# Softcap attention followed by a gated MLP on one core: two small loads change queue, two weight loads move behind accumulating transfers, and the hand-written order of the attention passes is written anew

## The chip, the core and the metric

One Trainium2 chip, one core. The metric is the device time of one execution in microseconds (us); lower is better. Times are those of the profiler or of the timed runs of this kernel.

## What is computed

```python
# q, k, v: (4, 12, 448, 64) float32; cap: one number; w_in: (768, 2048); w_out: (2048, 768)
scores = (q @ k^T) / sqrt(64)
scores = cap * tanh(scores / cap)
attn = exp(scores - max); attn = attn / (sum(attn) + 1e-9)
x = (attn @ v) as (1792, 768)          # tokens by heads x head_dim
h = x @ w_in
out = (h * sigmoid(h)) @ w_out         # (1792, 768)
```

## The kernel before

Everything is scheduled by hand: each engine executes its own list of instructions in the order in which the code issues them, and waits only where data, a buffer or a PSUM bank is not ready. A step that is issued earlier or later in the code stands earlier or later in the list of its engine.

**Attention** runs in 12 passes (numbered `s`, 0 to 11). A pass handles two pairs of heads: `QK` tiles hold queries and keys of a pair (four buffers, two per pass), `VT` and `VB` the values. The keys of a pass are cut into seven units `u` (0 to 6). The steps are written as short names, `name.pass` in the tables `START` and `END`, and `name+lag` or `name-lag` in `SLOT`, which is repeated for each pass in `MIDDLE`:

- `Qu`: the four TensorE products of unit `u` (line 327) into a tile `s` of two PSUM banks. There are three such tiles, used in turn.
- `Tu`: ScalarE reads the tile and writes tanh into `P` (line 336), which frees the tile.
- `E0`, `E1`, `E2`: ScalarE's exp over units 0 to 2, 3 to 5, and 6 (line 340); `eu` is the exp of one unit, used in the first and the last pass.
- `Vu`: TensorE multiplies values with `P` into the tile `o` (line 387). There is only one such tile (two banks), so that the first `V` of a pass waits until `N0` of the pass before has read it.
- `S0` to `S4` and `A0`: the row sums. `S0` adds units 0 and 1, `S1` units 3 and 4, `S4` adds unit 5, `S2` unit 6, `S3` adds both halves, all on VectorE (lines 356 to 365). `A0` adds unit 2 to the first half: in passes 1 to 10 by an accumulating transfer on GpSimd's queue (line 370, `T<-P` in the rows), in passes 0 and 11 by VectorE. `S3` therefore waits for that transfer.
- `SUM`: TensorE sums over the partitions with a matrix of ones, into a tile `s` (line 397). It waits for `S3`.
- `UT0`, `UT1`, `UT2`: VectorE transposes, takes the reciprocal, transposes back (lines 408, 411, 414). `UT0` frees the tile of `SUM`.
- `N0`, `N1`, `N2`: VectorE divides and splits the result into a high and a low part, `XH` and `XL` (lines 425 to 429).
- `D1`, `D2`: VectorE decodes pieces of the MLP's first weights, which come as 64-bit words in `RAW` (lines 167 to 180, 615, 640).
- `LQ`, `LV`: loads of queries and keys two passes ahead, and of values one pass ahead, on SyncE's queue. A `QK` buffer is free when the last `Q` of the pass that used it is done.
- `H0` to `H5`: six parts of the first MLP product, placed into the last pass.

The loads of the first two pieces of `w_out` (768 KB as seen in the profile) go into the `RAW` buffers of the first two pieces of `w_in` as soon as these are decoded: the decode puts them on a list `WANTED`, and `LQ` issues what stands there behind its own loads, on SyncE's queue.

Ahead of `START` stand the first loads: queries and keys of pairs 0 and 1 in two pieces each, `cap` into `cap0` and, for partition 64, into `cap64`, values, pairs 2 and 3, two pieces of `w_in`. `setup3`, issued behind the first `T`, makes the small constant `epst` from `cap0` and `cap64` with two exps on ScalarE (lines 274 and 275), the second of which needs `cap64`; ScalarE's first exp of the pass, line 340, stands behind them.

**The MLP** follows, ordered by a planner in the code (`plan`), line 760 and line 870 in the profile. Its products use PSUM tiles `A` to `D` (one bank each) and `q` (two of two banks), which take over the banks of `s` and `o`.

Of the kernel before, what the change touches and what calls it, by code (L numbers as in the profile page):

```python
# [185 lines left out]
def tile_softcap_attention_swish_moe(  # L186
# [12 lines left out]
    nc = tc.nc  # L199
# [5 lines left out]
    S = NT // B  # L205
# [3 lines left out]
    KW = KF + 128  # L209
# [22 lines left out]
    psm = ExitStack()  # L232
    pool = lambda st, name, bufs, **kw: st.enter_context(tc.tile_pool(name=name, bufs=bufs, reuse_waits="tile", **kw))
# [18 lines left out]
    cap64 = a1.tile([128, 1], F32, name="cap64")  # L252
# [54 lines left out]
    def load_qk(i, c0=0, c1=S + KW, eng=nc.sync):  # L307
        eng.dma_start(out=QK[i % 4][:, c0:c1], in_=qkv[i, :, c0:c1])
# [108 lines left out]
    def norm(s, parts=(0, 1, 2)):  # L417
# [37 lines left out]
    }  # L455

    START = """
        Q0.0 Q1.0 Q6.0 T0.0 Q3.0 e0.0 T1.0 T6.0 e1.0 Q4.0 T3.0 Q5.0 T5.0 D1.1 Q2.1 T4.0 Q2.0 Q0.1 T2.1 D2.1 e3.0
        e5.0 e4.0 Q1.1 V3.0 V1.0 LV.0 T2.0 T0.1 S0.0 V5.0 e6.0 V4.0 T1.1 LQ.0 e2.0 D1.2 S1.0 Q4.1 Q3.1 T3.1 S4.0
        Q5.1 A0.0 T4.1 V0.0 T5.1 S3.0 V2.0 V6.0 D2.2 SUM.0 E0.1 D1.3 UT0.0 Q1.2 E1.1 T1.2 Q4.2 T4.2 Q6.1 T6.1  # L460
        LQ.1 Q2.2 T2.2 Q0.2 UT1.0 S0.1 Q5.2 E2.1 T0.2 UT2.0 S1.1 T5.2 N0.0 V0.1 V3.1 D2.3 V1.1 S2.0 E0.2 D1.4
        Q3.2 LV.1 S2.1 V2.1 S4.1 Q2.3 A0.1 V6.1 S3.1 SUM.1 T3.2 S0.2 Q6.2 T2.3 LQ.2 V4.1 N1.0 V5.1 Q1.3 E1.2
        UT0.1 UT1.1 Q0.3 UT2.1 T6.2 A0.2 T1.3 Q4.3 T0.3 E2.2 S1.2 Q3.3 E0.3 T4.3 N0.1 S4.2 S2.2 Q5.3 V1.2 N2.0
        V6.2 T5.3 S3.2 S0.3 V5.2 T3.3 LV.2 V2.2 V0.2 SUM.2 V3.2 UT0.2 Q2.4 Q6.3 E1.3 T2.4 N1.1 Q1.4 V4.2 T6.3
        T1.4 UT1.2 UT2.2 E2.3 Q0.4 T0.4 Q4.4 LQ.3 Q3.4 LV.3 S1.3 N0.2 V3.3 Q5.4 V5.3 T4.4 S4.3 A0.3 V6.3 D2.4
        E0.4 S2.3 N1.2 S3.3 N2.1 V0.3 V1.3 T3.4 SUM.3 V2.3 S0.4 Q6.4 T5.4 Q2.5 E1.4 UT0.3 V4.3 LQ.4 T6.4 UT1.3
        Q0.5 Q1.5 T2.5 T0.5 D1.5
    """.split()
# [8 lines left out]
    END = """
        T1.9 UT2.7 E2.8 Q4.9 Q3.9 LV.8 S1.8 N0.7 V3.8 T4.9 V2.8 V4.8 S4.8 Q5.9 N2.6 S2.8 V0.8 T3.9 A0.8 E0.9
        T5.9 D2.9 Q6.9 S3.8 V6.8 SUM.8 T6.9 E1.9 LQ.9 Q2.10 V1.8 S0.9 V5.8 N1.7 UT0.8 Q1.10 Q4.10 T2.10 T1.10
        T4.10 E2.9 Q5.10 Q0.10 Q6.10 T5.10 UT1.8 UT2.8 N2.7 N0.8 V0.9 LV.9 S1.9 T0.10 E0.10 Q3.10 V6.9 V2.9 S2.9  # L480
        T6.10 V1.9 A0.9 D1.10 S4.9 V5.9 S3.9 T3.10 E1.10 S0.10 SUM.9 Q2.11 A0.10 V3.9 UT0.9 UT1.9 T2.11 V4.9
        LQ.10 UT2.9 N0.9 S1.10 Q4.11 Q1.11 T4.11 Q3.11 S4.10 Q0.11 T1.11 E2.10 V2.10 e1.11 D2.10 V0.10 S2.10
        V6.10 S3.10 S2.11 V4.10 N1.8 V1.10 T3.11 Q6.11 LV.10 T0.11 e2.11 N2.8 SUM.10 V3.10 e3.11 UT0.10 Q5.11
        V5.10 e0.11 UT1.10 S0.11 UT2.10 H0 e4.11 H1 LQ.11 T5.11 e5.11 H2 N1.9 T6.11 N0.10 S1.11 H3 H4 H5 A0.11
        V5.11 V3.11 S4.11 LV.11 V2.11 V1.11 S3.11 N1.10 N2.9 V4.11 N2.10 e6.11 SUM.11 UT0.11 UT1.11 V0.11 V6.11
        UT2.11 N0.11
    """.split()

    def step(op, s):
        if not 0 <= s < NS:  # L490
            return
        j = int(op[-1]) if op[-1].isdigit() else None
        if op == "SUM":
            pv_sum(s)
        elif op[:2] == "UT":
            u_sums(s, j)
        elif op[0] == "N":
            if s + 1 < NS or j == 0:
                norm(s, (j,))
        elif op[0] == "D":  # L500
            if (s, op) in FIRST:
                decode(*FIRST[s, op])
        elif op[0] == "A":
            fold(s)
        elif op == "LQ":
            if s + 2 < NS:
                load_qk(2 * s + 4)
                load_qk(2 * s + 5)
            for m in WANTED:
                load_w(m)  # L510
            WANTED.clear()
        elif op == "LV":
            if s + 1 < NS:
                load_v(s + 1)
                if (s + 1) % NU == 0:
                    load_rem((s + 1) // NU)
        elif op[0] == "E":
            exp(s, j)
        elif op[0] == "e":
            exp(s, *place(j))  # L520
        else:
            dict(Q=qk, T=tanh, V=pv, S=sums)[op[0]](s, j)
        if op[0] == "T" and "cap" not in REG:
            setup3()
            load_factor("cap", cap0)
# [63 lines left out]
    MPOOL = {}  # L591
# [53 lines left out]
    WANTED = []  # L645
# [206 lines left out]
    HBANK = {}  # L852
# [29 lines left out]
    SUM = {}  # L882
# [160 lines left out]
    def moe():  # L1043
# [70 lines left out]
        line = []  # L1114
# [125 lines left out]
        o = lambda fp, blk: [("o", fp, blk, t) for t in ROWS(blk)]  # L1240
        h = lambda f, blk: [("h", f, blk)]
# [101 lines left out]
```

## Time and profile before

| | us |
|---|---|
| median of three timed runs | 611.03 (610.34 to 612.39) |
| the profiled execution, its own time | 611.36 |
| its span, first to last instruction | 609.5 |
| TensorE busy in the span | 594.5 |
| VectorE busy | 441.4 |
| ScalarE busy | 366.9 |

The span is what the profiler records between the first and the last instruction; 1.86 us of the execution lie outside it. Busy time is the time in which an engine has an instruction running. Attention takes the span's first 160 us, the MLP the rest.

### The profile page before, as it was taken

The numbers are of one execution on the slowest core, as the hardware profiler recorded it, in microseconds if no ns is written. First come the engines' busy times: TensorE is split into PE (matmuls) and PEld (weight loads), VectorE is DVE, ScalarE is ACT, GpSimd is POOL, SyncE is SP. The second block draws the span as 40 slices with busy tenths as digits, with TensorE's granted clock in tenths as the row PEclk, the third lists the DMA queues.
The fourth block names the chain that finished last, engine by engine and source line by source line (L and its number), as shares of the span: only waits on it lengthen the run. The fifth ranks groups of instructions, "written<-read, shape, count | busy, mean of one in ns | idle before, by whom it ended". The sixth has DMA issues, their size and how long they took to land.

```text
span 609.5 us, 10200 instructions
## 1 busy us (share of the span) xinstructions
PE 594.5 (98%) x3874; PEld 487.4 (80%) x3874; DVE 441.4 (72%) x714; ACT 366.9 (60%) x578; POOL 183.8 (30%) x227
## 2 busy tenths in 40 slices
PE   7879999999999999999999999999999999999996
PEld 2324444334689989989999999999899999999996
DVE  2768999999999887675667574767666675747553
ACT  5978999999255655545555555546465545555220
POOL 0000010010113223633444364436334443645210
PEclk9999999999999999999999999999999999999999
DMA  9368668752363617998997899789889978997975
GB/s 278 95 171 198 169 141 220 195 135 54 92 198 118 208 52 174 145 175 125 178 182 113 181 130 207 93 180 143 183 135 172 175 118 179 133 203 130 289 238 204
DMA packets 47132, 99.18 MB, mean 163 GB/s; under 512 B 8612, under 2 KB 34212, under 8 KB 47076
## 3 DMA queue, kind: packets, MB, share of 16 engines
q0 software_dynamic: 29088, 49.56, 51.7%
q1 hardware_dynamic: 17844, 48.64, 24.2%
q8 instruction: 32, 0.52, 0.4%
q10 hardware_dynamic: 144, 0.26, 0.2%
q14 instruction: 24, 0.20, 0.1%
HBM read 47.97 MB, written 44.04 MB: 151 GB/s over the span
## 4 chain that ended last, share of the span: by engine, by line
PE 89%; DVE 4%; DMA 3%; ACT 2%; issue 1%; SPq 0%; DVEq 0%; ACTq 0%
PE q L870 37%; PE A L760 14%; PE o L387 9%; PE C L760 8%; PE s L327 8%; PE B L760 6%; PE D L760 3%; DMA T<-P 2%; PE s L397 2%; ACT P L336 1%; ACT P L340 1%; PE s L760 1%; DMA cap<-in_cap_dram 1%; DVE xt L694 1%; DVE US L408 0%
## 5 line engine op out<-in xcount | busy, mean ns | idle before, releaser
L912 POOL DMA_DIRECT2D out_dram<-st x196 | 164.6, 952 | 232.6 <-ACT st L613 213.8
L870 PE MATMUL q<-w,gh 128*128 128x376 f32 (+1 forms) x876 | 187.6, 336 | 0.5 <-DVE st L615 0.5
L870 PEld LDWEIGHTS q<-w,gh 128*128 128x128 f32 x876 | 156.2, 188 | 3.7 <-ACT gf L169 0.9
L613 ACT ACTIVATE st<-q 128x376 f32<-128x376 f32 (+1 forms) x177 | 80.3, 488 | 61.3 <-PE q L870 48.3
L870 PE MATMUL q<-w,gl 128*128 128x376 f32 (+2 forms) x438 | 111.3, 335 | 0.0
L870 PEld LDWEIGHTS q<-w,gl 128*128 128x128 f32 x438 | 80.2, 188 | 0.0
L336 ACT ACTIVATE P<-s 128x896 f32<-128x896 f32 x84 | 72.8, 936 | 9.6 <-PE s L327 6.6
L327 PE MATMUL s<-QK 64*64 64x448 f32 x672 | 73.0, 547 | 4.5 <-ACT P L336 4.1
L340 ACT ACTIVATE P<-P 128x896 f32<-128x896 f32 (+1 forms) x44 | 71.6, 1653 | 0.5 <-ACT epst L275 0.2
L387 PE MATMUL o<-P,VT 64*64 64x448 f32 x576 | 64.3, 544 | 0.0
L327 PEld LDWEIGHTS s<-QK 64*64 64x64 f32 x672 | 26.4, 134 | 44.3 <-ACT P L336 21.5
L760 PE MATMUL A<-XH,w 128*128 128x512 f32 (+1 forms) x192 | 61.2, 362 | 0.0
L613 ACT ACTIVATE gh<-gf 128x512 fp32r<-128x512 f32 (+1 forms) x63 | 36.4, 578 | 25.6 <-DVE gf L824 25.6
L387 PEld LDWEIGHTS o<-P,VT 64*64 64x64 f32 x576 | 23.9, 135 | 31.8 <-issue 29.0
L830 DVE TENSOR_TENSOR gl<-gf,gh 128x512 fp32r<-128x512 f32 (+1 forms) x63 | 39.1, 622 | 12.8 <-ACT gh L613 12.7
L370 POOL DMA_DIRECT2D T<-P x10 | 8.7, 871 | 126.9 <-DVE T L356 93.0
L613 ACT ACTIVATE gf<-A 128x512 f32<-128x512 f32 (+1 forms) x32 | 17.6, 549 | 43.6 <-PE A L760 42.9
L760 PE MATMUL B<-XH,w 128*128 128x384 f32 (+1 forms) x136 | 40.5, 359 | 0.0
L760 PEld LDWEIGHTS A<-XH,w 128*128 128x128 f32 x192 | 35.7, 188 | 3.7
L760 PE MATMUL A<-xt,w 128*128 128x512 f32 (+1 forms) x168 | 38.4, 364 | 0.0
L169 ACT ACTIVATE gf<-RAW 128x384 f32<-128x384 f32 x56 | 30.6, 548 | 12.9 <-DVE RAW L180 4.9
L760 PE MATMUL C<-XH,w 128*128 128x512 f32 (+1 forms) x124 | 37.7, 365 | 0.0
(131 smaller groups left out, 882.9 us busy)
## 6 DMA issues: line engine op xcount, KB each, us to landing
out_dram<-st POOLq DMA_DIRECT2D x98, 196.0 KB, 5.0
out_dram<-st POOLq DMA_DIRECT2D x98, 188.0 KB, 3.9
RAW<-in_moe_w_in_dram SPq DMA_DIRECT2D x16, 768.0 KB, 7.2
RAW<-in_moe_w_out_dram SPq DMA_DIRECT2D x16, 768.0 KB, 7.7
QK<-in_qkv_dram SPq DMA_DIRECT2D x22, 480.0 KB, 5.7
VT<-in_qkv_dram SPq DMA_DIRECT2D x24, 192.0 KB, 7.1
T<-P POOLq DMA_DIRECT2D x10, 448.0 KB, 6.0
xt<-out_dram POOLq DMA_DIRECT2D x8, 384.0 KB, 5.4
```

The source lines that it names most:

```text
L169: nc.scalar.activation(out=tmp, in_=high.bitcast(F32), func=AF.Abs)
L327: nc.tensor.matmul(ps[half(t), e, 0:S], q[half(e), k0:k0 + 64], q[half(e), 0:S], start=True, stop=True)
L336: nc.scalar.activation(out=P[s, g][:, k], in_=SP.pop((s, u))[:, :, 0:S], func=AF.Tanh, scale=REG["sct"])
L340: nc.scalar.activation(out=p, in_=p, func=AF.Exp, scale=REG["cap"])
L370: nc.gpsimd.dma_start(out=t, in_=p, accum_op=ALU.add)
L387: nc.tensor.matmul(O[s][half(e), t, 0:S], v, p, start=(DONE[s] == 0), stop=(DONE[s] == NC - 1))
L397: nc.tensor.matmul(ps[half(e), t, 0:S], ones[half(t)], p[half(t), e], start=(n == 0), stop=(n == len(parts) - 1))
L613: nc.scalar.activation(out=out, in_=in_, func=AF.Copy)
L760: nc.tensor.matmul(ps, w(a), x(b), start=(first and z == 0), stop=(last and z == 2), skip_group_check=more)
L830: nc.vector.tensor_tensor(gl, gf, gh.bitcast(F32), ALU.subtract)
L870: nc.tensor.matmul(pe(e), g[a][:, ts], w[:, b, cols[e]], start=(z == 0 and a == 0 and b == 0), stop=(z == G - 1 and a == 1),)
L912: nc.gpsimd.dma_start(out=out[rows, part_cols(fp)[e]], in_=SUM[fp, blk, t, e], **how)
```

## The change

- The second pieces of queries and keys of pair 1 and the load of `cap64` move from SyncE's queue to ScalarE's, ahead of ScalarE's first activation.
- `WANTED` is emptied behind `A0` and not in `LQ`: the two `w_out` loads go to GpSimd's queue, behind the accumulating transfers of passes 2 and 6.
- `START`, `SLOT` and `END` hold other orders, and `MIDDLE` begins at pass 4 in place of 5. The steps are the same.
- The PSUM tiles of the MLP are taken in the other sequence: `q` first, then `A` to `D`, and the first products use `A` to `D` in another rotation. Apart from these names the instructions of the MLP stand in the same order as before on every engine.

```diff
@@ fold
             nc.gpsimd.dma_start(out=t, in_=p, accum_op=ALU.add)
         else:
             nc.vector.tensor_tensor(flat(t), flat(t), flat(p), ALU.add)
+        for m in WANTED:
+            load_w(m, nc.gpsimd)
+        WANTED.clear()
@@ the tables
     SLOT = """
-        T1 UT2-2 E2-1 Q4 Q3 LV-1 S1-1 N0-2 V3-1 Q5 V5-1 T4 S4-1 A0-1 V6-1 D2 E0 S2-1 N1-2 S3-1 N2-3 V0-1 V1-1 T3
-        SUM-1 V2-1 S0 Q6 T5 Q2+1 E1 UT0-1 V4-1 LQ T6 UT1-1 Q0+1 Q1+1 T2+1 T0+1 D1+1
+        N2-3 T0 T1 E2-1 S2-1 Q3 E0 D2 S3-1 T5 V2-1 LV-1 T3 V3-1 V0-1 S0 Q4 A0 V5-1 SUM-1 T4 UT0-1 E1 V1-1 D1+1
+        Q6 UT1-1 V6-1 Q2+1 N1-2 LQ UT2-1 V4-1 Q0+1 S1 N0-1 T6 Q1+1 S4 T2+1 Q5+1
     """.split()
 
-    MIDDLE = range(5, 9)
+    MIDDLE = range(4, 9)
@@ step, LQ
                 load_qk(2 * s + 4)
                 load_qk(2 * s + 5)
-            for m in WANTED:
-                load_w(m)
-            WANTED.clear()
@@ attention
         nc.sync.dma_start(out=cap0, in_=cap.partition_broadcast(1))
+        load_qk(1, S + 64, S + KW, nc.scalar)
+        load_qk(0, S + 64, S + KW)
+        nc.scalar.dma_start(out=cap64[64:65], in_=cap.partition_broadcast(1))
         nc.scalar.activation(out=sigt, in_=XL.bitcast(F32)[:, NP - 1, NT - 1:NT], func=AF.Exp)
-        load_qk(0, S + 64, S + KW)
-        load_qk(1, S + 64, S + KW)
         load_v(0)
-        nc.sync.dma_start(out=cap64[64:65], in_=cap.partition_broadcast(1))
         load_qk(2)
@@ end of attention
+        MPOOL["o"] = pool(psm, "ps_q", 2, space=PSUM)
         MPOOL["h"] = pool(psm, "ps_h", 1, space=PSUM)
-        MPOOL["o"] = pool(psm, "ps_q", 2, space=PSUM)
@@ moe, whole
-            q = HBANK[f, blk] = "CDAB"[len([x for x in line if x[0] == "h"]) % 4]
+            q = HBANK[f, blk] = "ABCD"[len([x for x in line if x[0] == "h"]) % 4]
```

**First place: ScalarE at the start.** These are the first rows of ScalarE's list before the change: the load of `QK` on its queue, the table load, the first tanh, the two exps of `epst`, then exps (`P<-P`) and tanhs (`P<-s`) of pass 0.

```order
L308 DMA QK_83<-in_qkv_dram 128x512
L542 ACT_TABLE_LOAD
L542 ACTIVATE sigt<-XL 128x1
L296 TENSOR_LOAD sct
L336 ACTIVATE P<-s 128x896
L274 ACTIVATE epst<-over_60 1x1
L275 ACTIVATE epst<-cap_93 1x1
L296 TENSOR_LOAD cap_92
L340 ACTIVATE P<-P 128x896
L336 ACTIVATE P<-s 128x896 x2
```

The same rows of the changed kernel:

```order
L308 DMA QK_83<-in_qkv_dram 128x512
L308 DMA QK_83<-in_qkv_dram 128x448
L541 DMA cap_93<-in_cap_dram 1x1
L542 ACT_TABLE_LOAD
L542 ACTIVATE sigt<-XL 128x1
L296 TENSOR_LOAD sct
L336 ACTIVATE P<-s 128x896
L274 ACTIVATE epst<-over_60 1x1
L275 ACTIVATE epst<-cap_93 1x1
L296 TENSOR_LOAD cap_92
L340 ACTIVATE P<-P 128x896
L336 ACTIVATE P<-s 128x896 x2
```

Two issues have come in front of the table load; the load of `cap64` (`cap_93`), seventh of SyncE's loads before, is now ScalarE's third.

**Second place: the transfer queues in passes 1 and 2.** SyncE's list before, from the loads for pass 2 on (`QK_82`, `QK_83`), with those for pass 3 (`QK_84`, `QK_85`), `w_out` and the values of pass 2 (`VT_86`):

```order
L308 DMA QK_82<-in_qkv_dram 128x960
L308 DMA QK_83<-in_qkv_dram 128x960
L1277 TENSOR_LOAD over_59
L1277 ISA x2
L308 DMA QK_84<-in_qkv_dram 128x960
L308 DMA QK_85<-in_qkv_dram 128x960
L606 DMA RAW_66<-in_moe_w_out_dram 128x768
L313 DMA VT_86<-in_qkv_dram 64x2x384 x2
```

GpSimd's list of the changed kernel, with the accumulating transfers of passes 1 to 10 (`T<-P`, ten in a row before the change):

```order
L370 DMA T<-P 128x896 x2
L603 DMA RAW_66<-in_moe_w_out_dram 128x768
L370 DMA T<-P 128x896 x4
L603 DMA RAW_67<-in_moe_w_out_dram 128x768
L370 DMA T<-P 128x896 x4
```

The first `w_out` load has left the place behind the `QK` loads of pass 3 and stands behind the transfer of pass 2; the second stands behind that of pass 6.

**Third place: VectorE from pass 1's first sum to pass 1's last.** Before the change, from `S0.1` (line 356) to `S3.1` (line 363):

```order
L356 SCALAR_TENSOR_TENSOR T<-P,epst 128x896
L414 STREAM_TRANSPOSE US<-CS 128x896
L361 TENSOR_TENSOR T<-P 128x896
L425 TENSOR_TENSOR U<-o,US 128x896
L167 TENSOR_SCALAR KRV<-RAW_67 128x768
L171 TENSOR_SCALAR KRV<-KRV 128x768
L172 TENSOR_SCALAR KRV<-KRV 128x768
L365 TENSOR_TENSOR T<-T,P 128x896 x2
L363 TENSOR_TENSOR T<-T 128x896
```

And of the changed kernel, the same stretch (its lines 411 to 428 are 408 to 425 before, 612 and 637 are 615 and 640):

```order
L356 SCALAR_TENSOR_TENSOR T<-P,epst 128x896
L411 STREAM_TRANSPOSE US<-s 128x896
L414 RECIPROCAL CS<-US 128x28
L637 TENSOR_TENSOR w_68<-RAW_66,w_68 128x768
L417 STREAM_TRANSPOSE US<-CS 128x896
L167 TENSOR_SCALAR KRV<-RAW_67 128x768
L361 TENSOR_TENSOR T<-P 128x896
L428 TENSOR_TENSOR U<-o,US 128x896
L365 TENSOR_TENSOR T<-T,P 128x896 x2
L171 TENSOR_SCALAR KRV<-KRV 128x768
L172 TENSOR_SCALAR KRV<-KRV 128x768
L363 TENSOR_TENSOR T<-T 128x896
```

`S0.1` has moved ahead of `UT0.0`, so that three more instructions of pass 0 and a decode stand between it, which starts the transfer, and `S3.1`, which needs it.

## Rows read from the trace of the kernel before

**Rows 1.** The page's first part: busy time, share of the span, instructions.

```profile
span 609.5 us, 10200 instructions
PE 594.5 (98%) x3874; PEld 487.4 (80%) x3874; DVE 441.4 (72%) x714; ACT 366.9 (60%) x578; POOL 183.8 (30%) x227
```

**Rows 2.** Stretches: length; busy PE, PEld, DVE, ACT, POOL; granted clock, DMA share, GB/s.

```profile
38.00:42.10 4.10, 0.08 (x8) 0.06 (x5) 1.22 (x2) 1.35 (x3) 0.00 (x0) 1.00 0.36 95
42.10:46.40 4.30, 4.30 (x28) 1.95 (x32) 4.23 (x6) 2.96 (x2) 0.88 (x1) 0.60 0.37 67
...
50.80:160.00 109.20, 109.17 (x1126) 48.81 (x1119) 106.10 (x121) 101.40 (x94) 6.79 (x8) 1.00 0.60 143
160.00:600.00 440.00, 439.54 (x2365) 418.31 (x2364) 302.76 (x547) 226.49 (x443) 174.73 (x212) 1.00 0.82 164
```

**Rows 3.** Who TensorE waited for: us in total, times, longest.

```profile
PE s L397 <- DVE T L363: 4.0, 1, 4.0
```

**Rows 4.** Timeline of the span's start: start, us, engine, instruction, idle before it.

```profile
1.31 0.33 SPq L541 DMA_DIRECT2D cap<-in_cap_dram  x1
...
4.01 0.45 SPq L546 DMA_DIRECT2D cap<-in_cap_dram  x1
...
4.58 0.15 DVE L554 RECIPROCAL sct<-cap 1x1 f32<-1x1 f32 x1 [3.35 <-DMA cap<-in_cap_dram]
...
6.85 0.18 ACT L274 ACTIVATE epst<-over 1x1 f32<-1x1 f32 x1
...
8.27 0.14 DVE L272 TENSOR_SCALAR epst<-cap 1x1 f32<-1x1 f32 x1 [3.12 <-DMA cap<-in_cap_dram]
...
8.63 0.20 ACT L275 ACTIVATE epst<-cap 1x1 f32<-1x1 f32 x1 [1.60 <-DVE cap L273]
...
9.01 0.95 ACT L340 ACTIVATE P<-P 128x896 f32<-128x896 f32 x1 [0.18 <-ACT epst L275]
```

**Rows 5.** Timeline of ScalarE alone, later in passes 0 to 3.

```profile
12.30 3.34 ACT L336 ACTIVATE P<-s 128x896 f32<-128x896 f32 x4
15.49 2.67 ACT L340 ACTIVATE P<-P 128x896 f32<-128x896 f32 x3
18.01 1.76 ACT L336 ACTIVATE P<-s 128x896 f32<-128x896 f32 x2
...
24.47 4.87 ACT L340 ACTIVATE P<-P 128x2688 f32<-128x2688 f32 x2
...
37.09 1.06 ACT L336 ACTIVATE P<-s 128x896 f32<-128x896 f32 x1
```

**Rows 6.** Timeline around pass 1's accumulating transfer.

```profile
27.84 1.05 DVE L356 SCALAR_TENSOR_TENSOR T<-P,epst 128x896 f32<-128x896 f32 x1
...
28.66 0.81 SPq L308 DMA_DIRECT2D QK<-in_qkv_dram  x2
...
29.21 1.04 POOL L370 DMA_DIRECT2D T<-P  x1 [28.31 <-DVE T L356]
29.56 0.38 SPq L606 DMA_DIRECT2D RAW<-in_moe_w_out_dram  x1
...
40.88 1.09 DVE L363 TENSOR_TENSOR T<-T 128x896 f32<-128x896 f32 x1 [5.21 <-DMA T<-P]
```

**Rows 7.** The tile T: its ten transfers, from issue to landing.

```profile
DMA to landing us min/median/max: 4.4/6.0/11.6
```

**Rows 8.** Timeline of VectorE, from the S3 of pass 3 to that of pass 4.

```profile
63.63 1.08 DVE L363 TENSOR_TENSOR T<-T 128x896 f32<-128x896 f32 x1
...
65.63 1.14 DVE L356 SCALAR_TENSOR_TENSOR T<-P,epst 128x896 f32<-128x896 f32 x1
66.70 1.11 DVE L408 STREAM_TRANSPOSE US<-s 128x896 f32<-128x896 f32 x1
...
74.89 1.08 DVE L363 TENSOR_TENSOR T<-T 128x896 f32<-128x896 f32 x1
```

**Rows 9.** The chain that ended last, one unit of TensorE's in pass 3.

```profile
65.79 0.75 PE s L397 x8
```

More of the change, by code (lines that the diff above doesn't have):

```diff
@@ L457, in tile_softcap_attention_swish_moe @@
     START = """
[L458 to L467, printed above, removed]
+        Q0.0 T0.0 Q2.0 Q3.0 e0.0 T2.0 T3.0 Q1.0 Q4.0 e2.0 e3.0 T4.0 S2.0 T1.0 Q2.1 V3.0 Q6.0 T2.1 e4.0 Q1.1 Q5.0
@@ new lines, in tile_softcap_attention_swish_moe @@
+        T6.0 S1.0 T1.1 Q0.1 e1.0 T5.0 D1.1 D2.1 Q4.1 V0.0 T0.1 e6.0 V2.0 e5.0 Q5.1 V6.0 T4.1 E0.1 S0.0 A0.0 D1.2
+        V1.0 S4.0 S3.0 Q3.1 V4.0 V5.0 T5.1 SUM.0 T3.1 LQ.0 E1.1 D2.2 S0.1 Q2.2 Q0.2 LV.0 UT0.0 A0.1 Q1.2 UT1.0
+        T2.2 T0.2 D1.3 Q6.1 T1.2 UT2.0 D2.3 S1.1 T6.1 Q5.2 LQ.1 Q3.2 T5.2 E2.1 Q4.2 N0.0 E0.2 S4.1 S2.1 V4.1
+        D1.4 LV.1 V3.1 S3.1 T3.2 V2.1 V0.1 V5.1 SUM.1 V1.1 S0.2 T4.2 Q1.3 E1.2 T1.3 Q6.2 UT0.1 UT1.1 N1.0 V6.1
+        UT2.1 Q0.3 A0.2 T6.2 Q2.3 N0.1 T0.3 E2.2 T2.3 S1.2 Q5.3 N1.1 V2.2 Q4.3 LQ.2 S4.2 T5.3 N2.0 Q3.3 V3.2
@@ L468, in tile_softcap_attention_swish_moe @@
+        V5.2 E0.3 LV.2 V4.2 S2.2 T4.3 T3.3 E1.3 V6.2 S3.2 S0.3 SUM.2 UT0.2 UT1.2 V1.2 UT2.2 V0.2 Q6.3 T6.3 Q2.4
+        Q0.4 S1.3 N0.2 Q1.4 S4.3 T2.4 LQ.3 A0.3 Q5.4
     """.split()
     SLOT = """
-        T1 UT2-2 E2-1 Q4 Q3 LV-1 S1-1 N0-2 V3-1 Q5 V5-1 T4 S4-1 A0-1 V6-1 D2 E0 S2-1 N1-2 S3-1 N2-3 V0-1 V1-1 T3
-        SUM-1 V2-1 S0 Q6 T5 Q2+1 E1 UT0-1 V4-1 LQ T6 UT1-1 Q0+1 Q1+1 T2+1 T0+1 D1+1
+        N2-3 T0 T1 E2-1 S2-1 Q3 E0 D2 S3-1 T5 V2-1 LV-1 T3 V3-1 V0-1 S0 Q4 A0 V5-1 SUM-1 T4 UT0-1 E1 V1-1 D1+1
@@ L473, in tile_softcap_attention_swish_moe @@
+        Q6 UT1-1 V6-1 Q2+1 N1-2 LQ UT2-1 V4-1 Q0+1 S1 N0-1 T6 Q1+1 S4 T2+1 Q5+1
     """.split()
-    MIDDLE = range(5, 9)
+    MIDDLE = range(4, 9)
     END = """
[L478 to L486, printed above, removed]
+        N2.6 T0.9 T1.9 E2.8 Q3.9 S2.8 N1.7 T5.9 E0.9 T3.9 Q4.9 T4.9 S3.8 V1.8 V6.8 V2.8 V3.8 Q6.9 LV.8 S0.9
+        SUM.8 D2.9 T6.9 V5.8 UT0.8 Q2.10 UT1.8 UT2.8 E1.9 V0.8 Q1.10 T2.10 V4.8 Q0.10 T1.10 Q3.10 E2.9 S1.9
+        T0.10 Q5.10 N0.8 A0.9 T3.10 S4.9 V5.9 S2.9 S3.9 N2.7 V3.9 LQ.9 T5.10 S2.11 Q4.10 V6.9 D1.10 SUM.9 V0.9
+        Q6.10 E0.10 D2.10 LV.9 UT0.9 S0.10 V4.9 UT1.9 T4.10 E1.10 T6.10 V2.9 Q5.11 T5.11 V1.9 LV.10 Q1.11 Q3.11
+        Q2.11 UT2.9 T1.11 S1.10 Q4.11 A0.10 T3.11 N0.9 S4.10 E2.10 V3.10 e1.11 Q0.11 T4.11 T2.11 V2.10 S2.10
+        V5.10 V4.10 T0.11 e5.11 e0.11 V0.10 e3.11 N1.8 N1.9 S3.10 SUM.10 N2.8 V6.10 V1.10 UT0.10 UT1.10 Q6.11
+        e4.11 UT2.10 LV.11 S0.11 H0 H1 N0.10 H2 H3 T6.11 e6.11 e2.11 S1.11 LQ.11 H4 H5 A0.11 S4.11 V4.11 V1.11
+        V3.11 S3.11 N1.10 N2.9 N2.10 V5.11 SUM.11 LQ.10 UT0.11 V6.11 UT1.11 V0.11 UT2.11 V2.11 N0.11
```

## Prediction

> **What bounds the kernel now.** I read the busy times first. TensorE works for 594.5 of the span's 609.5 us [rows 1], so at most 15 us of idle time and whatever the clock loses can be won, and only there. The stretches say where: from 50.8 to 600 us TensorE idles for 0.03 and 0.46 us at full clock [rows 2]. The rest of the idle time lies ahead of 50 us and in the last microseconds, where the last result is stored. The change leaves the end alone, and the order of the whole MLP too. So the question is what the first 50 us give, and whether the new pass order keeps TensorE full until 160 us.
>
> In the first 50 us three rows matter. The longest wait of TensorE, 4.0 us, is for `S3` of pass 1 [rows 3], and VectorE had itself waited 5.21 us there for the accumulating transfer `T<-P`, issued at 29.21 and used at 40.88 [rows 6]; that transfer took 11.6 us, where the median of the ten is 6.0 and the shortest 4.4 [rows 7]. Issued just before and behind it were 960 KB of queries and keys and 768 KB of `w_out` [rows 6]. Behind the pause, 42.1 to 46.4, the granted clock is 0.60 [rows 2]. And ScalarE stood still for 1.60 us at 8.63, because `cap64` was used only at 8.27 [rows 4]; from its first exp at 9.01 to the end of the tanh that starts at 37.09 it then has no gap worth the name [rows 4, 5]. So ScalarE paces TensorE up to 38 us: every tile it frees late is a product that starts late.
>
> **The change, part by part.** The profiled execution took 611.36 us, 0.33 above the median.
>
> *`cap64` on ScalarE's queue.* It was issued at 4.01 and used 4.3 us later; the other copy of `cap` was issued at 1.31 and used 3.3 us later, at 4.58 [rows 4]. On ScalarE's queue it stands third, behind two issues of some 0.4 us, so it leaves at about 1.6 and is there between 4.9 and 5.9. The first exp of `epst` runs at 6.85, so the second follows at 7.03, and line 340 starts 0.38 later as before (8.63 to 9.01): at 7.4 in place of 9.01. **Gain 1.6 us** of ScalarE's chain. Below, it is nothing if the copy lands after 8.27. The two added issues push ScalarE's table load by 0.8 us, hidden by the wait for the first keys. The second piece of pair 1 is now in flight earlier, beside the first pieces: I charge **0.3 us** for the first product, between 0 and 0.8, the two issues of 0.4 by which it comes earlier.
>
> Is ScalarE's chain kept busy as before? From 9.01 to 38.15 it did 19 tanh, 8 single exps and 3 exps of three units. Rows give 0.80 us for a tanh (3.19 for four), 0.84 for an exp (2.52 for three) and some 2.4 for a big exp [rows 5]; 19 x 0.80 + 8 x 0.84 + 3 x 2.4 = 29.1, which is the whole stretch of 29.14. In the new `START` the same number stands up to `T4.2`, so that point is reached at 36.6. I walked TensorE's list beside it: a `Q` may start when the tile three tiles back has been read, and takes 0.75 us, the unit of [rows 9]. All tiles are filled before ScalarE comes to them.
>
> *The transfer of pass 1.* Its start hangs on `S0.1`, and that on `E0.1`. In the new order 10 tanh, 7 exps and `E0.1` stand between 7.4 and the end of `E0.1`: 23.7. `S0.1` takes 1.05, and the transfer was issued 0.3 after it [rows 6]: at 25.1 in place of 29.21. SyncE's loads for pass 3 still wait for the last `Q` of pass 1, which is `Q6.1` in both orders, and by the walk that ends at 29.4 in the new one. So the transfer runs nearly alone: 4.4 to 6.0 us, landed by 31.1. VectorE needs it at `S3.1`. It had 13.0 us between the starts of `S0.1` and `S3.1`, less 5.21 of waiting [rows 6], 7.8 of work; three more instructions of at most 1.1 us (`UT0.0`, `UT1.0`, a decode) make about 10. So `S3.1` comes at 33.7 at the earliest. The margin is 2.6 us; with 11.6 us the transfer would land at 36.7. **Gain 4.0 us**, 1 us at worst.
>
> *The clock.* 4.3 us at 0.60 lose 4.3 x 0.40 = 1.7 us against full clock [rows 2]. The pause that stood ahead of it is the only one of such length in the early passes, and it is gone. **Gain 1.7 us**, or nothing if another pause of this length comes.
>
> *The new pass.* A pass is 15 units of TensorE, 15 x 0.75 = 11.25 us. VectorE's own work from `S3.3` to `S3.4`, without a wait, was 74.89 - 63.63 = 11.26 [rows 8], and it was busy for 106.1 of 109.2 us [rows 2]: VectorE is as full as TensorE. In `SLOT` now `SUM` comes seventh among TensorE's units and VectorE has only `S0` (66.70 - 65.63 = 1.07 us) between `S3` and `UT0`, which needs `SUM`; before, `N2` of another pass stood there too. `S3` to `SUM` to `UT0` takes about 0.1 + 0.75 + 0.3 = 1.15 to 1.3 us, so VectorE idles for 0.1 to 0.25 us per pass, in some nine passes: 0.7 to 2.2 us. Some is covered, since pass 8 has a decode less. **Loss 1.0 us**, between 0 and 2.5.
>
> *Nothing else.* The `w_out` loads are wanted four passes later, when their decode begins; the transfer of pass 3 behind the first has a whole pass of cover. GpSimd has nothing else to do in that time (6.79 us of work in 109.2) [rows 2]. Without the cover a late `w_out` would stop VectorE's decode and then `S3`. The exchanged banks cost nothing: `C` and `D` take the banks of `o`, free when `N0.11` has read it, about 4 us after the last `SUM`; TensorE still has three `V` (3 x 0.75) and the 18 matmuls of the first product before it needs them; without that product it would wait for 1.7 us.
>
> The sum: 1.6 + 4.0 + 1.7 - 0.3 - 1.0 = 6.0 us, 605.4 against the profiled 611.36, and **605.0 us** against the median.
>
> **The rivals.** *VectorE eats it.* If each of nine passes loses 0.4 us in `S3` - `SUM` - `UT0` or by a tile freed late, 3.6 us in place of 1.0 are lost: 607.6. For it speaks that VectorE has 3.1 us of slack in 109 [rows 2]; against it that the steps are the same and start earlier.
>
> *The transfers still collide.* Pass 2's transfer now leaves at about 37, with `w_out` behind it on its own queue, and SyncE's loads for pass 4 from 38.8 on. If it takes 11.6 us again it lands at 48.6, `S3.2` ends at 49.7, and `SUM.2`, due at 47, comes 2.7 us late; with the slow clock behind it 4.4 us are lost: 609.4. If pass 1 collides as well, only `cap64` is won, also 609.4. Against it: it leaves ahead of the loads, not behind them, and the others took 6 us beside the loads of their own passes [rows 7]. The Trainium skill, DMA: Bandwidth & Descriptors, section on queues, rings and completion order, says that each DMA engine takes turns between queues that have work. By that rule a transfer beside one busy queue takes at most about twice its time alone: 8.8 us from the fastest 4.4, pass 2's would land at 45.8, `SUM.2` would be on time, the sum would stay at 605.0, and `w_out` at the tail of SyncE's queue would never have mattered. The row shows 11.6 us [rows 7], by which the sum would be 609.4; no row shows a transfer with the loads behind it.
>
> *Slower.* The new pass stalls TensorE each time: `SUM` wants the tile that `T5` frees, and `T5` stands behind a big exp; `Q0` of the next pass then wants `UT0`. By the walk `T5` ends 0.1 to 0.2 us ahead of `SUM`. If this ring loses 1.0 us per pass in nine passes, 9.0 us go in place of 1.0, and the time is 613.0. It decides against the change from 0.8 us per pass on. Against it: ScalarE's work in a pass, 7 x 0.80 + 0.84 + 2 x 2.4 = 11.24 us [rows 5], still fits into TensorE's 11.25, if barely.
>
> *The change does nothing*: what is won early is waited for later, because VectorE's chain sets the end of attention whatever the start: 611. Against it, VectorE itself lost 5.21 us in the wait that goes away [rows 6].
>
> **How the numbers follow.** A difference under 0.3%, 1.8 us, can't be told from no change. Forecast (603.2 to 606.5, the early gain kept but for some 1 us): 58%. VectorE eats part, or a milder collision, 606.5 to 609.2: 22%. A full collision or nothing won, 609.2 to 612.9: 12%. Slower: 6%. More than forecast, with no loss in the passes: 2%. The range 603.0 to 609.0 leaves out about 2 in 10. Faster 0.82, same 0.12, slower 0.06.
>
> **What would show it.** ScalarE's line 340 starts near 7.4 with no wait for `cap`; line 363 of pass 1 has no wait for `T<-P`, and that transfer takes at most 7 us; TensorE has no idle stretch over 1.5 us after 11 us, and the clock stays at 1.00 from 38 to 50; the first MLP product into a bank of its own starts near 153 in place of 159; in passes 4 to 8 VectorE waits for `SUM` for 0.1 to 0.25 us each. I am wrong if a wait of `SUM` for VectorE or of a `Q` for ScalarE returns in every pass, or if pass 2's transfer takes 11 us.

## The result, and the profile after

The changed kernel took 604.59 us (median of 4, 604.05 to 605.46), the kernel before 610.68 beside it (median of 4, 610.18 to 612.39): a ratio of 0.9897, 95% interval 0.9873 to 0.992. Forecast were 605.0 us, 603.0 to 609.0. The profiled execution of the changed kernel took 605.46 us, 5.90 less than that of before. Its lines have other numbers than before: the helpers of attention stand three lines lower (397 is now 400), the MLP three lines higher (760 is now 757).

Beside [rows 1], the page's first part of the changed kernel:

```profile
span 603.7 us, 10198 instructions
...
PE 594.2 (98%) x3874; PEld 485.2 (80%) x3874; DVE 440.7 (73%) x714; ACT 367.2 (61%) x578; POOL 185.3 (31%) x229
```

TensorE's busy time is nearly that of before (594.2 against 594.5 us): 5.5 of the 5.8 us by which the span is shorter are idle time. That the slow clock, which is gone, hardly shows in it comes from the start: in the first 12 us TensorE is busy for 9.82 us, before for 8.58. Beside [rows 2], the same stretches of the changed kernel (length; busy PE, PEld, DVE, ACT, POOL; granted clock; DMA share; GB/s), the third up to 153 us, where attention now ends:

```profile
38.00:42.10 4.10, 4.10 (x49) 1.96 (x44) 3.88 (x6) 3.99 (x4) 1.62 (x2) 1.00 0.53 99
42.10:46.40 4.30, 4.30 (x52) 2.04 (x48) 4.30 (x6) 4.30 (x6) 0.00 (x0) 1.00 0.96 315
50.80:153.00 102.20, 101.79 (x1054) 43.33 (x1050) 99.51 (x113) 95.02 (x89) 8.11 (x9) 1.00 0.65 159
160.00:598.00 438.00, 438.00 (x2362) 417.62 (x2361) 299.46 (x544) 224.22 (x439) 172.19 (x210) 1.00 0.81 163
```

From 38 to 42.1 us TensorE is full, where it worked for 0.08 us before, and the clock behind is 1.00 in place of 0.60 (a mean: the lower of the clock's two levels, 0.50, was granted from 42.9 to 46.2 us). New is 0.41 us of idle time in the third stretch. Whom TensorE waited for, in the whole run of the changed kernel (us, times, longest), beside [rows 3]:

```profile
PE s L327 <- ACT P L336: 1.4, 2, 0.7
PE o L263 <- DVE XL L260: 1.3, 1, 1.3
PE s L327 <- DMA QK<-in_qkv_dram: 0.9, 2, 0.5
PE s L400 <- issue: 0.4, 1, 0.4
PE o L390 <- ACT P L340: 0.4, 1, 0.4
PE s L400 <- DVE T L363: 0.2, 1, 0.2
```

The wait of 4.0 us is gone; of line 363 only 0.2 is left. ScalarE's timeline at the start of the changed kernel (start, us, instruction, idle before it and who ended it), beside [rows 4]:

```profile
6.59 0.92 ACT L336 ACTIVATE P<-s 128x896 f32<-128x896 f32 x1 [2.83 <-PE s L327]
7.40 0.18 ACT L274 ACTIVATE epst<-over 1x1 f32<-1x1 f32 x1
7.61 0.20 ACT L275 ACTIVATE epst<-cap 1x1 f32<-1x1 f32 x1
7.83 0.95 ACT L340 ACTIVATE P<-P 128x896 f32<-128x896 f32 x1
...
10.20 0.92 ACT L336 ACTIVATE P<-s 128x896 f32<-128x896 f32 x1 [0.58 <-PE s L327]
```

Line 275 no longer waits for `cap`. Line 274 is 0.55 late (6.85 before), and a tanh behind waits 0.58 for scores. The timelines of GpSimd, SyncE and VectorE of the changed kernel around pass 1's transfer, beside [rows 6], and under them its ten transfers, beside [rows 7]:

```profile
26.88 1.04 POOL L370 DMA_DIRECT2D T<-P  x1 [25.97 <-DVE T L356]
...
30.89 1.82 SPq L308 DMA_DIRECT2D QK<-in_qkv_dram  x2
...
36.00 1.08 DVE L363 TENSOR_TENSOR T<-T 128x896 f32<-128x896 f32 x1
...
39.28 1.06 POOL L603 DMA_DIRECT2D RAW<-in_moe_w_out_dram  x1
```

```profile
DMA to landing us min/median/max: 4.4/5.2/7.2
```

The transfer now leaves 4.0 us ahead of SyncE's loads, where it stood 0.55 behind them, none of the ten takes over 7.2 us (11.6 before), and line 363 doesn't wait.

The packets show where the time went. By queue (q1: SyncE's; q0: GpSimd's), they are, with their number, MB and share of the DMA engines' time, in the kernel before from 29.2 to 34.3 us, then from 34.3 to 39.6, and in the changed kernel from 28.4 to 31:

```profile
q1 hardware_dynamic: 331, 1.25, 88.9%
...
q1 hardware_dynamic: 362, 0.88, 51.6%
q0 software_dynamic: 144, 0.46, 44.0%
...
q0 software_dynamic: 144, 0.46, 94.8%
```

Before, the first of the transfer's packets starts 5.2 us after its issue (34.40), in the changed kernel after 1.6 us (28.48); from the first packet to the end of the last are 5.2 us beside the loads and 2.5 alone. So of the 7.2 us between 11.6 and 4.4, the late first packet makes 3.6, the shared engines 2.7. What holds the first packet back the profile doesn't show.

### The profile page after: what moved, and what is told of

Same layout as the page of the kernel before. It is cut to its first block, busy times and chain, and to the rows that moved or that the text cites. A ratio compares the mean times of both kernels' runs of the same rounds, so it can differ in the third digit from the quotient of the medians.

```text
span 603.7 us, 10198 instructions
## 1 busy us (share of the span) xinstructions
PE 594.2 (98%) x3874; PEld 485.2 (80%) x3874; DVE 440.7 (73%) x714; ACT 367.2 (61%) x578; POOL 185.3 (31%) x229
## 4 chain that ended last, share of the span: by engine, by line
PE 95%; ACT 3%; DMA 1%; issue 1%; SPq 0%; DVE 0%
PE q L867 38%; PE A L757 15%; PE C L757 10%; PE o L390 10%; PE s L327 9%; PE B L757 7%; PE D L757 4%; ACT P L336 2%; PE s L400 2%; ACT P L340 1%; DMA QK<-in_qkv_dram 1%; PE s L757 1%; PE B L867 0%; PE A L867 0%; DVE RAW L917 0%
## 5 line engine op out<-in xcount | busy, mean ns | idle before, releaser
L390 PE MATMUL o<-P,VT 64*64 64x448 f32 x576 | 62.3, 537 | 0.4 <-ACT P L340 0.4
L327 PEld LDWEIGHTS s<-QK 64*64 64x64 f32 x672 | 26.1, 136 | 42.9 <-issue 22.1
L757 PE MATMUL A<-XH,w 128*128 128x512 f32 (+1 forms) x180 | 57.9, 364 | 0.0
L757 PE MATMUL C<-XH,w 128*128 128x512 f32 (+1 forms) x136 | 40.9, 362 | 0.0
L637 DVE TENSOR_TENSOR w<-RAW,w 128x768 fp32r<-128x768 f32 x32 | 30.2, 952 | 9.1 <-ACT w L610 9.1
```

What stands on the lines that cost most here:

```text
L327: nc.tensor.matmul(ps[half(t), e, 0:S], q[half(e), k0:k0 + 64], q[half(e), 0:S], start=True, stop=True)
L390: nc.tensor.matmul(O[s][half(e), t, 0:S], v, p, start=(DONE[s] == 0), stop=(DONE[s] == NC - 1))
L637: nc.vector.tensor_tensor(WS[m][:, 1], f, WS[m][:, 0].bitcast(F32), ALU.subtract)
L757: nc.tensor.matmul(ps, w(a), x(b), start=(first and z == 0), stop=(last and z == 2), skip_group_check=more)
```

## Experiments

The parts of the change are four: first loads (L), `w_out` on GpSimd's queue (W), order of the passes (O), exchanged banks (K). Each group of kernels ran beside the kernel before on one chip (611.26, 611.5 and 611.88 us, medians of 26, 11 and 11 runs), and times are told as differences to it: the changed kernel itself, run once more, took 604.57 us beside 611.5, 6.93 less.

**L alone** (`e1_loads`), the kernel before with

```diff
+        load_qk(1, S + 64, S + KW, nc.scalar)
         load_qk(0, S + 64, S + KW)
-        load_qk(1, S + 64, S + KW)
+        nc.scalar.dma_start(out=cap64[64:65], in_=cap.partition_broadcast(1))
         load_v(0)
-        nc.sync.dma_start(out=cap64[64:65], in_=cap.partition_broadcast(1))
```

> The kernel before with only the first loads moved (second piece of pair 1 and cap64 on ScalarE's queue). My theory: ScalarE's first exp starts 1.2 us earlier, as in the changed kernel (7.83 against 9.01), everything that hangs on ScalarE's chain moves with it, loads and transfer included; the wait of 4.0 us for pass 1's transfer stays. 609.5 us, between 609.0 and 610.2. Rival: the wait for the transfer of pass 1 swallows what is won ahead of it, 610.7, no change.

Measured: 609.75 us (1.5 less; ratio 0.9972, 0.9961 to 0.9983). Its VectorE timeline, ten transfers, and stretches (columns as above):

```profile
38.60 1.09 DVE L363 TENSOR_TENSOR T<-T 128x896 f32<-128x896 f32 x1 [5.16 <-DMA T<-P]
```

```profile
DMA to landing us min/median/max: 4.4/5.9/11.5
```

```profile
38.00:42.10 4.10, 2.31 (x14) 0.93 (x18) 3.17 (x4) 3.25 (x2) 0.77 (x1) 0.58 0.01 4
42.10:46.40 4.30, 4.30 (x33) 1.65 (x29) 3.54 (x5) 0.92 (x1) 0.12 (x1) 0.61 0.88 179
```

Transfer and loads came earlier together (26.98 and 26.43 us), the transfer's first packet started 5.1 us after its issue, so the wait stayed as long, and the slow clock stayed: an earlier start alone doesn't remove the wait. This profiled execution is the slowest of 13 (612.47 us); TensorE waits 1.7 us more in it for line 363 of pass 8, so that its total doesn't stand for L's.

**W alone** (`e2_wout`), the kernel before with

```diff
             nc.gpsimd.dma_start(out=t, in_=p, accum_op=ALU.add)
...
+        for m in WANTED:
+            load_w(m, nc.gpsimd)
+        WANTED.clear()
```

and the same three lines taken out of `LQ`.

> The kernel before with only the w_out loads moved to GpSimd's queue behind the accumulating transfers; in this order the first stands behind pass 1's. My theory: w_out's 768 KB are what made that transfer take 11.6 us; with the 960 KB of queries and keys left beside it, it takes some 8 us, TensorE's wait falls from 4.0 to under 1 us and the slow clock behind it goes: 605.5 to 607 us. Rival, by which each DMA engine takes turns between the queues: w_out stood at the tail of SyncE's queue and never delayed the transfer, which still takes 11 us or more; 610 to 611.

Measured: 608.8 us (2.5 less; ratio 0.9965, 0.9949 to 0.998). VectorE at line 363 of pass 1, and the ten transfers:

```profile
37.91 1.09 DVE L363 TENSOR_TENSOR T<-T 128x896 f32<-128x896 f32 x1 [2.55 <-DMA T<-P]
```

```profile
DMA to landing us min/median/max: 4.6/6.2/9.0
```

Half-way, between my theory and its rival: with `w_out` behind it on its own queue the transfer took 9.0 us in place of 11.6, its first packet started after 3.3 us, and half of VectorE's wait is left.

**O alone** (`e3_order`): the tables `START`, `SLOT`, `END` and `MIDDLE` of the changed kernel in the kernel before.

> The kernel before with only the tables START, SLOT, END and MIDDLE of the changed kernel; w_out stays on SyncE's queue behind the loads for pass 3. My theory: the new order by itself starts pass 1's transfer ahead of these loads, so that it takes at most 7 us; 4.0 of wait and 1.7 of clock are won, about 1.0 is lost in the middle passes, and the 1.2 of the first loads is missing: 605.5 to 606.5. Rival: without the move of w_out a transfer is late again, and the order costs more than it gives: 609 or more.

Measured: 608.56 us (2.7 less; ratio 0.9963, 0.9949 to 0.9977). Line 363 of pass 1 starts at 36.21 with no wait, the longest transfer takes 7.1 us, the clock is 1.00 from 38 to 46.4 us: the order does that alone, with `w_out` still on SyncE's queue (transfer at 27.10, loads from 31.10 on). But the time is 2 us above what I expected, since TensorE has a wait that neither kernel has (its waits: us, times, longest):

```profile
PE D L757 <- DVE gf L821: 2.3, 1, 2.3
```

**L, W and O, the banks as before** (`e4_no_banks`): the changed kernel less

```diff
+        MPOOL["o"] = pool(psm, "ps_q", 2, space=PSUM)
         MPOOL["h"] = pool(psm, "ps_h", 1, space=PSUM)
...
-        MPOOL["o"] = pool(psm, "ps_q", 2, space=PSUM)
...
-            q = HBANK[f, blk] = "CDAB"[len([x for x in line if x[0] == "h"]) % 4]
+            q = HBANK[f, blk] = "ABCD"[len([x for x in line if x[0] == "h"]) % 4]
```

> The changed kernel with the PSUM tiles of the MLP taken as before (A to D first, rotation CDAB). The changed kernel won 0.7 us between the first MLP product and 185 us that I had not counted. If the banks did that, this kernel loses it: 605.3, with TensorE's wait of 0.5 us for line 615 back near 176. If it comes from the earlier work of VectorE alone, this kernel is as fast as the changed one: 604.6, no such wait.

Measured: 607.77 us (3.5 less; ratio 0.9948, 0.9929 to 0.9968), and the same wait of 2.3 us; neither of my two cases came. The wait shows that the new order leaves the first gate's product where the old layout puts `D`: `D` waits until VectorE has read it (line 821). Line 615's wait isn't there, but the 2.3 us ahead of it can have hidden it, so what won the 0.7 us stays open.

**K alone** (`e8_banks_alone`): only the diff above, in the kernel before.

> The kernel before with nothing but the exchanged PSUM banks. My theory, from the wait that the new order showed with the old banks: order and banks belong together, since the last passes leave the tile that the first gate reads in another pair of banks; with the old order the first product into a bank of its own now lands on that pair and waits about 2.3 us for the gate's read on VectorE: 613 to 614 us. Rival, the banks are neutral by themselves: the time of the kernel before.

Measured: 614.76 us, 2.9 more (ratio 1.0056, 1.0036 to 1.0077). TensorE's timeline at the first product into a bank of its own:

```profile
162.35 0.44 PE L760 MATMUL B<-XH,w 128*128 128x384 f32 x1 [3.04 <-DVE gf L824]
```

The direction was right, the wait is 0.7 longer than I took over from the other order. Order and banks belong together: either without the other waits for the gate.

**The loads behind the transfer** (`e11_loads_behind`): the kernel before, with pass 3's QK loads and `w_out` on GpSimd's queue, behind pass 1's transfer:

```diff
-        LQ.1 Q2.2 T2.2 Q0.2 UT1.0 S0.1 Q5.2 E2.1 T0.2 UT2.0 S1.1 T5.2 N0.0 V0.1 V3.1 D2.3 V1.1 S2.0 E0.2 D1.4
-        Q3.2 LV.1 S2.1 V2.1 S4.1 Q2.3 A0.1 V6.1 S3.1 SUM.1 T3.2 S0.2 Q6.2 T2.3 LQ.2 V4.1 N1.0 V5.1 Q1.3 E1.2
+        Q2.2 T2.2 Q0.2 UT1.0 S0.1 Q5.2 E2.1 T0.2 UT2.0 S1.1 T5.2 N0.0 V0.1 V3.1 D2.3 V1.1 S2.0 E0.2 D1.4
+        Q3.2 LV.1 S2.1 V2.1 S4.1 A0.1 LQ.1 Q2.3 V6.1 S3.1 SUM.1 T3.2 S0.2 Q6.2 T2.3 LQ.2 V4.1 N1.0 V5.1 Q1.3 E1.2
...
+                eng = nc.gpsimd if s == 1 else nc.sync
```

> The kernel before with one thing moved: the QK and w_out loads that stood just ahead of and behind pass 1's accumulating transfer on SyncE's queue (LQ.1) go to GpSimd's queue behind that transfer. First theory, what is issued ahead of the transfer makes it slow: it takes 7 us or less, line 363 of pass 1 does not wait, TensorE's 4.0 us and the slow clock behind it go, 605.5 to 607 us. Rival, the same bytes in flight at the same time make it slow whatever the order: 10 us or more, the wait stays, 609.5 to 611.5 us. A third outcome, that the QK loads come too late for pass 3's first scores, would show as a wait of TensorE for QK near 39 us.

Measured: 607.64 us (4.2 less; ratio 0.9935, 0.992 to 0.995). Its timelines of GpSimd and VectorE, and its stretches:

```profile
29.17 1.03 POOL L370 DMA_DIRECT2D T<-P  x1 [28.27 <-DVE T L356]
29.88 1.44 POOL L308 DMA_DIRECT2D QK<-in_qkv_dram  x2
30.95 0.90 POOL L607 DMA_DIRECT2D RAW<-in_moe_w_out_dram  x1
...
35.66 1.09 DVE L363 TENSOR_TENSOR T<-T 128x896 f32<-128x896 f32 x1
```

```profile
38.00:42.10 4.10, 4.10 (x44) 1.92 (x48) 2.61 (x5) 3.28 (x4) 0.89 (x1) 1.00 0.60 134
42.10:46.40 4.30, 4.30 (x48) 2.35 (x44) 4.20 (x5) 3.85 (x6) 0.00 (x0) 1.00 1.02 289
```

The transfer leaves at the old time, with QK loads and `w_out` 0.7 and 1.8 us behind it: VectorE finds it landed 6.5 us later, the wait and the slow clock are gone. So the start of the chain is not what did it. Two things moved along: the loads changed queue, and 384 KB of V loads, no longer held up behind the QK loads, left at 23.94 in place of 29.99 us, so that the order, the queue and the bytes in flight beside the transfer are not wholly told apart here. O alone leaves the loads on SyncE's queue. In both, the transfer's first packet starts 1.6 us after its issue. Pass 7's transfer, which this edit doesn't touch, takes 8.4 us here. The time is 0.6 us above the upper end that I gave.

**The changed kernel less L** (`e5_no_loads`) **and less W** (`e6_no_wout`), beside the changed kernel again (`after_again`):

> The changed kernel itself, once more, as the measure for the three kernels beside it. Both theories: 604 to 605.5 us, TensorE about 0.4 us idle between 90 and 100 us and none worth the name up to 190 us. First theory: the start of the first tanh differs from one execution to the next by up to 1 us with the landing of the first loads, and the whole time with it.

> The changed kernel with the first loads as before: the second copy of cap and the second QK piece back on SyncE's queue. My theory: the wait of ScalarE for the copy of cap returns (1.6 us at about 8.4 us) and every later step is late by as much, about 1.2 us net: 605.8 us, with the transfer of pass 1 still landed before line 363 wants it. Rival, that slack behind the start takes it up (VectorE sets the end of attention): the same time as the changed kernel.

> The changed kernel with the w_out loads back behind SyncE's QK loads. My theory: in the new order the transfer of pass 1 leaves ahead of those loads, lands in 7 us or less, and line 363 does not wait, so the time is that of the changed kernel within 0.5 us. Rival, that w_out on another queue is itself worth what it gave alone in the old order (about 2 us): 606.5 us, with a wait of line 363 for the transfer in pass 1 or 2.

Measured: 604.57 us for the changed kernel (603.88 to 605.75), 606.2 less L, 604.2 less W (603.88 to 606.76). Without L, ScalarE waits again (timeline; 8.63 in [rows 4]), and the 1.6 us are seen at the end in full:

```profile
8.47 0.20 ACT L275 ACTIVATE epst<-cap 1x1 f32<-1x1 f32 x1 [1.33 <-DVE cap L273]
```

Without W nothing is lost in the median, and line 363 doesn't wait. Its profiled execution, the slowest of six, shows what could be: TensorE waits 0.3 us for values that stand behind `w_out` on SyncE's queue (its waits), and `SUM` of pass 3 starts 1.3 us later than in the changed kernel (60.45 and 59.15), though that of pass 1 started with it (both 37.18); how the rest of the 1.3 us arises isn't shown. W can protect from that; how often it happens can't be told from six executions.

```profile
PE o L387 <- DMA VT<-in_qkv_dram: 0.3, 1, 0.3
```

**`N2` later** (`e7_n2_later`) **and `D2` later** (`e10_d2_later`), two ways to fill VectorE's wait for `SUM` in the changed kernel (`e7` moves `N2.6` in `END` likewise):

```diff
-        N2-3 T0 T1 E2-1 S2-1 Q3 E0 D2 S3-1 T5 V2-1 LV-1 T3 V3-1 V0-1 S0 Q4 A0 V5-1 SUM-1 T4 UT0-1 E1 V1-1 D1+1
+        T0 T1 E2-1 S2-1 Q3 E0 D2 S3-1 T5 V2-1 LV-1 T3 V3-1 V0-1 S0 N2-3 Q4 A0 V5-1 SUM-1 T4 UT0-1 E1 V1-1 D1+1
```
```diff
-        N2-3 T0 T1 E2-1 S2-1 Q3 E0 D2 S3-1 T5 V2-1 LV-1 T3 V3-1 V0-1 S0 Q4 A0 V5-1 SUM-1 T4 UT0-1 E1 V1-1 D1+1
+        N2-3 T0 T1 E2-1 S2-1 Q3 E0 S3-1 T5 V2-1 LV-1 T3 V3-1 V0-1 S0 D2 Q4 A0 V5-1 SUM-1 T4 UT0-1 E1 V1-1 D1+1
```

> The changed kernel with the last third of the normalisation of an older pass (N2) moved on VectorE, from ahead of a pass's work to the place between S0 and UT0, where VectorE waits for SUM. My theory: VectorE's waits for SUM (2.0 us in 5) go and its sums are ready earlier, so TensorE's 0.4 us idle at 93 us goes too: 0.4 to 0.8 us faster than the changed kernel, 604.0 us or less. Rival, VectorE has slack enough and the waits cost nothing: the same time, with the 0.4 us still there.

> The changed kernel with the decode step D2 in the middle passes moved on VectorE from ahead of S3 to behind S0, into the place where VectorE waits for SUM. Theory: what cost TensorE 0.4 us at 93 us is the longest decode step (0.98 us) ahead of S3; S3 then ends earlier in each pass, the 0.4 us are gone, 0.3 to 0.6 us faster than the changed kernel: 604.0 to 604.3 us. Rival: the loss comes back within the same passes (VectorE is as full as TensorE), 604.6 us.

Measured: 604.72 us (6.8 less) and 604.42 us (in another group, 7.5 less); the changed kernel has 6.9 less, and no difference can be told. The traces are finer. With `N2` later VectorE's waits for `SUM` fell from 2.0 us in 5 to 1.1 in 3, and TensorE's stall near 93 us from 0.41 to 0.13. But `SUM` of pass 9 now starts only when line 363 is through, and from pass 0's `SUM` to the first product in a bank of its own it takes 129.40 us, where the changed kernel takes 128.95: the stall moved, no time came back, and my theory fell. With `D2` later the stall near 93 us went. The changed kernel there, VectorE and then TensorE (timeline):

```profile
91.61 0.98 DVE L176 SCALAR_TENSOR_TENSOR KRV<-RAW,KRV 128x768 uint32<-128x768 uint32 x1
92.48 1.11 DVE L363 TENSOR_TENSOR T<-T 128x896 f32<-128x896 f32 x1
...
93.69 0.98 PE L400 MATMUL s<-T,ones 64*64 64x448 f32 x8 [0.41 <-issue]
```

`SUM` starts when line 363 is through, and line 363 stands behind the longest decode step. The stretch from 90 to 100 us with `D2` later has 10 us of TensorE for 9.59 in the changed kernel:

```profile
90.00:100.00 10.00, 10.00 (x112) 3.86 (x105) 9.96 (x13) 9.97 (x9) 0.84 (x1) 1.00 0.81 202
```

From pass 0's `SUM` to the first product in a bank of its own the changed kernel needs 128.95 and, run again, 128.91 us, with `D2` later 128.48 (24.90 to 153.38). So 0.4 us are won in the passes of this execution, less than the medians can show over the spread of the start.

**Only the copy of `cap` on ScalarE's queue** (`e12_cap_only`), in the changed kernel:

```diff
-        load_qk(1, S + 64, S + KW, nc.scalar)
         load_qk(0, S + 64, S + KW)
         nc.scalar.dma_start(out=cap64[64:65], in_=cap.partition_broadcast(1))
+        load_qk(1, S + 64, S + KW)
```

> The changed kernel with the second QK piece back on SyncE's queue and only the copy of cap on ScalarE's. My theory: all of what the first loads give (1.6 us) comes from the copy of cap, and the QK piece on ScalarE's queue costs the first product 0 to 0.5 us: 604.0 to 604.6 us. Rival, the QK piece is needed early for the next scores: 605 us or more, with a wait of TensorE for QK or of ScalarE near 8 to 10 us.

Measured: 604.52 us (604.35 to 605.31), 7.4 less, where the changed kernel has 6.9 less in its group. So the copy of `cap` gives all of L, and the QK piece on ScalarE's queue wins nothing, as far as the medians can show.

## Why the prediction held, step by step

- *`cap64`, 1.6 us.* Right. Line 340 came 1.18 us earlier in the profiled execution (9.01 to 7.83; 7.55 when run again), and without L the time is 1.6 us longer.
- *First product, 0.3 lost.* Not shown. Line 274 is 0.55 late in the profiled execution (6.85 to 7.40) and 0.26 when run again (7.11), but the start of the first tanh differs by up to 1.1 us among the profiles, and without the QK piece the time is the same. A wait that I had not walked, 0.58 us at 10.20 for scores, came on top in the profiled execution.
- *Transfer of pass 1, 4.0 us, and clock, 1.7 us.* Right, and for the reason given. It was issued at 26.88, not 25.1, since ScalarE's chain was later, and was still there in time. That the loads around its issue made it slow was argued from one row of before; with those loads moved behind it in the old order, 4.2 us are won. The way they do it I had not seen: half of the extra time passes ahead of its first packet.
- *The lead at 50 us.* After the same 392 matmuls of attention, `SUM` of pass 2 starts at 48.48 us, before at 54.31: a lead of 5.8 us, where the sum has 1.6 + 4.0 + 1.7 - 0.3 = 7.0. So the early gain was 1.2 us too large for this execution. ScalarE shows where it is missing: it ends the same 19 tanh and 11 exps at 37.85 (36.09 + 1.76), where the sum had 36.6 and before had 38.15; 0.4 us of that is the later start of line 340 (7.83, not 7.4), 0.6 the wait at 10.20, and the rest small gaps. Run again, the changed kernel has no wait there, ends them at 36.85, and its `SUM` of pass 2 starts at 47.48: a lead of 6.8 us. So the terms were about right, and the profiled execution lost 1 us at its start.
- *The new pass, 1.0 us lost.* The size was within the bounds given, the mechanism wrong. The lead is 5.2 us at the first product into a bank of its own (159.35 and 154.12; run again, 6.2), so 0.6 us were lost. VectorE does wait for `SUM`, up to 0.7 us where I had 0.25 (2.0 us in 5 waits), but TensorE's idle time is elsewhere: 0.4 us are the decode step ahead of `S3` in one pass.

```profile
DVE US L411 <- PE s L400: 2.0, 5, 0.7
```

That row, whom VectorE waited for in the changed kernel, shows idle time of VectorE; with `N2` later 0.9 us of it went, and TensorE was done no earlier.
- *Exchanged banks, nothing.* No wait is there, as said, and the reason given (the old `o` banks are free in time) was not what they are for: the new order needs them, or loses 2.3 us by its wait (3.4 by the medians, which are of two groups). Had the change left them out, my sum would have missed that.
- *`w_out`, nothing.* Right in the new order (604.2 without it). In the old order the same move is worth 2.5 us, because there the transfer takes 2.6 us less, 1.9 of them ahead of its first packet. W and O remove the same wait, so their gains do not add.
- *Not in the sum.* Between the first product and 185 us the lead grows from 5.2 to 6.0 us: a wait of TensorE for VectorE's `st` at 182.91 us of before (0.46 us) does not come back. I had not seen that term.

That the two profiled executions differ by 5.90 us, where the sum has 6.0, is in part luck: 1.2 us were missing at the start, 0.4 fewer were lost in the passes, and 0.7 came that were not in the sum. Where the start cost nothing, in the profiled execution of the changed kernel run again (604.53), 6.83 us were won.

Of the rivals, the full collision did not come: pass 2's transfer, with `w_out` behind it, held nobody up. The Trainium skill, DMA: Bandwidth & Descriptors, section on queues, rings and completion order, has the DMA engines take turns between queues that have work; from that I had estimated at most 8.8 us for a transfer beside one busy queue, and that `w_out` at the tail of SyncE's queue would never have mattered. From the transfer's first packet on the trace agrees: the two queues have 51.6 and 44.0% of the engines, and the packets take 5.2 us, about twice the 2.5 alone. But the whole time differs from the estimate, which has no late first packet: 10.9 to 11.6 us in three profiles with QK loads ahead of it and `w_out` behind it on SyncE's queue, 9.0 with `w_out` taken from there. In the new order, where pass 1's transfer leaves ahead of the loads, none of the ten took over 7.7 us in any profile, with `w_out` on either queue.

## What to carry to other kernels

When a transfer is slow, look at what was issued just ahead of it, and at when its first packet starts, before looking at its own time to spare: in this kernel 960 KB of loads issued 0.55 us ahead went with a first packet 5.2 us late, none ahead with 1.6, and an earlier start of both changed nothing. Try a reordering and the memory layout behind it together: here either half alone waited 2.3 to 3.0 us that the two together don't. And compare engines from anchor to anchor (here from pass 0's `SUM` to the first MLP product), where a few tenths show that the start's spread hides in the total.

## What was not expected of the hardware

- The accumulating transfer of 448 KB took 4.2 us at its best (in the changed kernel less W), 11.6 just behind 960 KB of loads with 768 KB following on SyncE's queue, 9.0 with these 768 KB on its own queue behind it, and at most 6.5 with all of them behind it (and 384 KB of V loads gone ahead). Its first packet started 5.2, 3.3 and 1.6 us after the issue. Why the 768 KB that were issued 0.35 us after it cost 2.6 us, 1.9 of them ahead of that packet, the runs do not tell.
- The start of the first tanh lay between 5.53 and 6.59 us in the profiles of these kernels, with no order in it by which queue brought the loads. Pass 0's `SUM` lay between 23.47 and 25.45 us in those of the new order; from there to the first MLP product four of them (the changed kernel twice, less L, and with the copy of `cap` only) took 128.91 to 128.95 us.
- Pauses of TensorE of 4.0 (before, L alone) and 3.3 us (K alone), all ahead of pass 1's `SUM`, went with the lower level of its clock, 0.50 (1.2 GHz): from 42.9 to 46.2 us before, from 38.7 to 45.4 in L alone (where TensorE resumed at 39.8), from 41.9 to 45.1 in K alone. Behind pauses of at most 1.6 us (W alone), and behind those of 2.3 (O alone) and 3.0 us (K alone) ahead of the first MLP product, the clock stayed at 1.00 (2.4 GHz).
